# Filter rows by the parity of k2 already in batch 0: the filter re-arranged on chip, and the weight sums moved to VectorE

## The chip, the cores and the metric

The kernel runs on one core of a Trainium2 chip. The metric is the device time of one execution in microseconds (us). TensorE (PE) multiplies matrices, VectorE (DVE) and ScalarE (ACT) work on elements and empty PSUM, GpSimd (POOL) does small table work and issues the transfers that convert float32 to bfloat16, and SyncE (SP) issues the other transfers.

## The reference

For each of 8 batches of 3008 rows and 256 channels: a real FFT along the rows, a product with a filter per frequency and channel, the inverse FFT, and then two dense layers with an exact GELU between them.

```python
X = np.fft.rfft(x, axis=1)                       # x: (8, 3008, 256)
Y = X * (filt_r + 1j * filt_i)[None, :, :]       # filters: (1505, 256)
y = np.fft.irfft(Y, n=x.shape[1], axis=1)
h = y.reshape(24064, 256) @ w_in                 # w_in: (256, 2048)
g = 0.5 * h * (1.0 + erf(h / sqrt(2.0)))
out = g @ w_out                                  # w_out: (2048, 256)
```

## The kernel before

The FFT of 3008 points is split as 47 x 64. The frequency is k1 + 47 k2, and of k1 only 0 to 23 are kept; the conjugates stand in for the rest. A filter tile F holds, per partition, one k2 in 0 to 63 (direct rows 0 to 31, mirrored rows 32 to 63), and along the free dimension real or imaginary part, k1 and channel.

Batch 0 goes through the steps c1, c1t, c2, c3, c3t, c4 at the start, without DRAM between them. Its rows in F are needed twice, once for the real part of the data (partitions 0 to 63) and once for the imaginary part (64 to 127); `dup_filters` copies them. Batches 1 to 7 go through s1 to s4, which pass through DRAM (R1, R2) between the steps and are woven into the stream of the dense layers. They want F arranged in another way: even and odd k2 apart (parity 0 in partitions 0 to 63, parity 1 in 64 to 127), each twice. For this the kernel before saves F to DRAM and loads it again in the other order.

The stream has 47 tiles of 512 rows, 16 slots each. Slot jc of tile t does `mm1` (two matmuls and a GELU) for tile t and a sixteenth of the second product (`mm2`, or `mm2_seven`, a seven-product scheme that needs `weight_sums`) for tile t-1. Steps of the next batch are put into slots by number.

```python
    def load_filters(self, k0, k):

        nc, D = self.nc, self.D
        for t, src in enumerate((self.filt_r, self.filt_i)):
            direct = _dram(src, k0 * D, [[NA * D, 32], [D, k], [1, D]])
            mirror = _dram(src, (NA - k0) * D, [[NA * D, 32], [-D, k], [1, D]])
            for q, a in enumerate((direct, mirror)):
                nc.gpsimd.dma_start(out=self.F[32 * q:32 * q + 32, t, k0:k0 + k, :], in_=a)

    def save_filters(self):
        self.Fd = self.dram.tile([64, 2, K1, 256], BF16, tag="Fd", name="Fd")
        self.nc.sync.dma_start(out=self.Fd, in_=self.F[0:64])

    def load_filters_again(self, k0, k):

        for par in range(2):
            for r in range(2):
                for q in range(2):
                    o = 64 * par + 32 * r + 16 * q
                    self.nc.sync.dma_start(out=self.F[o:o + 16, :, k0:k0 + k, :],
                                           in_=self.Fd[32 * q + (par ^ q):32 * q + 32:2, :, k0:k0 + k, :])

    def dup_filters(self, eng, k0, k):
        for k in range(k0, k0 + k, 2):
            o, i = (self.F[r:r + 64, :, k:k + 2, :].rearrange("p t a b -> p t (a b)") for r in (64, 0))
            (eng.copy if eng is self.nc.scalar else eng.tensor_copy)(out=o, in_=i)

    # ...
    def table_2_parities(self):
        t = self.T2.rearrange("p k r (s j e) -> p k r s j e", s=2, e=2)
        for par in range(2):
            for q in range(2):
                self.nc.gpsimd.tensor_copy(out=self.T2p[:, :, par, :, q, :], in_=t[:, :, :, q, :, par ^ q])

    # ...
    def s1(self, b, c):

        nc = self.nc
        if c == 0:
            self.st[b, "R1"] = self.dram.tile([NB, 48, 256], BF16, tag="R1", name="R1")
        a = self.pa.tile([128, 2, 4, 256], BF16, tag="a", name="a_sb")
        x = self.st[b, "x"]
        ps = [[self.bank("ps_s1", "h" if i == h == 0 else "f") for h in range(2)] for i in range(2)]
        for i in range(2):
            for r in range(2):
                for h in range(2):
                    w = 8 * c + 4 * r + 2 * i
                    nc.tensor.matmul(ps[i][h][64 * r:64 * r + 64, :], lhsT=self.T1s[64 * h:64 * h + NA],
                                     rhs=x[64 * h:64 * h + NA, w:w + 2, :], start=True, stop=True)
        for i in range(2):
            for h in range(2):
                self._evac(a[:, h, 2 * i:2 * i + 2, :].rearrange("p a b -> p (a b)"), ps[i][h], "act" if h else False)
        o = self.st[b, "R1"].rearrange("n q c -> q n c")
        for r in range(2):
            for h in range(2):
                w = HB * h + 8 * c + 4 * r
                nc.sync.dma_start(out=o[:, w:w + 4, :], in_=a[64 * r:64 * r + 48, h])

    def r1(self, b, c):
        bt = self.pb.tile([128, 6, 256], BF16, tag="b", name="b_sb")
        self.st[b, "b", c] = bt
        v = self.st[b, "R1"].rearrange("n (r k) c -> (n r) k c", r=2)
        self.nc.sync.dma_start(out=bt, in_=v[:, 6 * c:6 * c + 6, :])


    def s2(self, b, p):
        nc = self.nc
        ps = self.bank("ps_s2")
        for i in range(2):
            k = 2 * p + i
            nc.tensor.matmul(ps[:, 256 * i:256 * i + 256], lhsT=self.T2p[:, k].rearrange("p a b c d -> p (a b c d)"),
                             rhs=self.st[b, "b", k // 6][:, k % 6, :], start=True, stop=True)
        w = self.st[b, "p", p] = self.pp.tile([128, 2, 512], BF16, tag="p12", name="p12")
        nc.vector.tensor_tensor(out=w, in0=ps.unsqueeze(1).to_broadcast([128, 2, 512]),

    # ... s3: matmuls over p, s3_out: results to DRAM (R2), r2: loads them, s4: last step, into the ring y
    def mm1(self, t, jc):
        nc = self.nc
        if jc == 0:
            self.st["g", t] = self.pg.tile([128, 16, TCH], FP16, tag="g", name="g_sb")
        ps = self.bank("ps_h", "h")
        o = 0
        for off, n in self.segs(t):
            for dc in range(2):
                nc.tensor.matmul(ps[:, o:o + n], lhsT=self.w_in_sb[:, dc, jc * 128:jc * 128 + 128],
                                 rhs=self.ring[:, dc, off:off + n], start=(dc == 0), stop=(dc == 1))
            o += n
        nc.scalar.activation(out=self.st["g", t][:, jc, :], in_=ps, func=AF.Gelu)

    # ...
    def weight_sums(self):

        w = self.w_out_sb.rearrange("p (i k) (n o) -> p k n i o", k=2, n=2)
        q, tt = self.w_sums, self.nc.gpsimd.tensor_tensor
        for o, a, b, op in ((q[:, 0], w[:, 0, 1], w[:, 0, 0], ALU.subtract), (q[:, 1], w[:, 1, 1], q[:, 0], ALU.add),
                            (q[:, 2], w[:, 1, 1], w[:, 0, 1], ALU.add), (q[:, 3], w[:, 1, 0], q[:, 1], ALU.subtract)):
            for i in range(0, 8, 2):
                tt(out=o[:, i:i + 2], in0=a[:, i:i + 2], in1=b[:, i:i + 2], op=op)
```

`table_4_all` makes, in 24 GpSimd products and sums of 96 x 376 elements, the table that s4 multiplies by; it needs `table_4_rows`, `weights_4` and `table_4_factors` before it. The start of the program and the schedule:

```python
    for k, n in ((0, 4), (4, 8), (12, 12)):
        m.load_filters(k, n)
    m.load_w_in()
    nc.gpsimd.memset(m.vt[:, :, 96, :], 0.0)
    m.dup_filters(nc.gpsimd, 4, 20)
    m.save_filters()
    # ... batch 0: c1 to c4; k1 = 0 to 3 duplicated on ACT and DVE; x of batch 1 and w_out loaded by GpSimd
    for b in range(1, B):
        hi = first(b)
        if b == 1:
            s1, n1, r1, s2, n2, group, r2, s4, n4 = 0, 4, 15, 25, 2.5, 12, 62, 70, 0.62
        else:
            s1, n1, r1, s2, n2, group, r2, s4, n4 = hi - 94, 3.7, hi - 80, hi - 71, 3.4, 14, hi - 25, hi - 17, 1
        unit = lambda p: s2 + group * (p // 4) + int(n2 * (p % 4))
        for u in range(16):
            put(s4 + int(u * n4), m.s4, b, u // 2, u % 2)
        for c in range(4):
            put(s1 + int(c * n1), m.s1, b, c)
            put(r1 if c < 3 else unit(3) + 1, m.r1, b, c)
            put(r2 if c < 3 else s4 + int(4 * n4) + 1, m.r2, b, c)
        for p in range(12):
            put(unit(p), m.s2, b, p)
            if p % 4 == 3:
                put(unit(p) + 3, m.s3, b, p // 4)
                put(unit(p) + 4, m.s3_out, b, p // 4, 1)
        if b + 1 < B:
            for i in range(8):
                put(unit(i + 2) if b > 1 else 25, m.load_next, b, i + 2, i // 2, i % 2)

    put(0, m.table_2_parities)
    put(1, m.table_u_pick, g)
    put(1, m.table_4_rows, g)
    put(1, m.weights_4, g)
    put(10, m.load_filters_again, 0, 8)
    put(16, m.load_filters_again, 8, 16)
    put(4, m.weight_sums)
    put(12, m.table_4_factors, g)
    put(14, m.table_u)
    put(15, m.table_4_all, g)
    # ... sums_1, sums_2, sums_3 for the seven-product scheme
    for s in range((NT + 1) * 16):
        t, jc = s // 16, s % 16
        for f, a in at.pop(s, ()):
            f(*a)
        if t >= 1:
            (m.mm2_seven if t - 1 in seven else m.mm2)(t - 1, jc)
        if t < NT:
            m.mm1(t, jc)
    assert not at
```

Of the kernel before, what the change touches and what calls it, by code (L numbers as in the profile page):

```python
# [18 lines left out]
NA, NB = 47, 64  # L19
# [11 lines left out]
class _Mix:  # L31
    def __init__(self, ctx, tc, x, filt_r, filt_i, w_in, w_out, out):
# [23 lines left out]
        self.T1 = c.tile([2 * NA, 96], BF16, name="T1")  # L56
        self.T2p = c.tile([128, K1, 2, 2, 2, 16], BF16, name="T2p")
        self.U = c.tile([128, 2, 2, HB], BF16, name="U")
# [29 lines left out]
    def load_filters(self, k0, k):  # L88

        nc, D = self.nc, self.D  # L90
        for t, src in enumerate((self.filt_r, self.filt_i)):
            direct = _dram(src, k0 * D, [[NA * D, 32], [D, k], [1, D]])
            mirror = _dram(src, (NA - k0) * D, [[NA * D, 32], [-D, k], [1, D]])
            for q, a in enumerate((direct, mirror)):
                nc.gpsimd.dma_start(out=self.F[32 * q:32 * q + 32, t, k0:k0 + k, :], in_=a)

    def save_filters(self):
        self.Fd = self.dram.tile([64, 2, K1, 256], BF16, tag="Fd", name="Fd")
        self.nc.sync.dma_start(out=self.Fd, in_=self.F[0:64])

    def load_filters_again(self, k0, k):

        for par in range(2):
            for r in range(2):
                for q in range(2):
                    o = 64 * par + 32 * r + 16 * q
                    self.nc.sync.dma_start(out=self.F[o:o + 16, :, k0:k0 + k, :],
                                           in_=self.Fd[32 * q + (par ^ q):32 * q + 32:2, :, k0:k0 + k, :])

# [95 lines left out]
    def signs(self, g):  # L205

        set_ = self.nc.vector.memset
        self.turn = [g.tile([128, 1], FP32, name=n) for n in ("turn_r", "turn_i")]
        for t, s in zip(self.turn, (-1.0, 1.0)):
            set_(t, s)  # L210
            for lo in (32, 96):
                set_(t[lo:lo + 32], -s)

        self.wtc = g.tile([128, 1], FP32, name="wtc")
        set_(self.wtc, 2.0)
        set_(self.wtc[0:4], 1.0)
# [14 lines left out]
    def unit_matrices(self, g, cols):  # L231
        ts = self.nc.vector.tensor_scalar
        self.eye, self.swap = (g.tile([128, 128], BF16, name=n) for n in ("eye", "swap"))
        sg, to = (g.tile([128, 1], FP32, name=n) for n in ("sg", "to"))

        ts(out=sg, in0=self.ri, scalar1=8.0, scalar2=-8.0 * TURNS - 1.0, op0=ALU.mult, op1=ALU.add)
        self.nc.vector.tensor_tensor(out=to, in0=self.p, in1=sg, op=ALU.add)
        ts(out=self.swap, in0=cols, scalar1=to, scalar2=sg, op0=ALU.is_equal, op1=ALU.mult)
        ts(out=self.eye, in0=cols, scalar1=self.p, scalar2=None, op0=ALU.is_equal)
# [6 lines left out]
    def table_2_swap(self, h):  # L246
        t2 = self.T2[:, 12 * h:12 * h + 12]
        for i in range(2):
            ps = self.bank("ps_sw", "n")
            self.nc.tensor.matmul(ps[:, 0:384], lhsT=self.swap, rhs=t2[:, :, 0, 32 * i:32 * i + 32],  # L250
                                  start=True, stop=True)
            self._evac(t2[:, :, 1, 32 * i:32 * i + 32], ps[:, 0:384].rearrange("p (k j) -> p k j", k=12),
                       "act", 1.0 - 2.0 * i)
# [56 lines left out]
    def table_2_parities(self):  # L310
        t = self.T2.rearrange("p k r (s j e) -> p k r s j e", s=2, e=2)
        for par in range(2):
            for q in range(2):
                self.nc.gpsimd.tensor_copy(out=self.T2p[:, :, par, :, q, :], in_=t[:, :, :, q, :, par ^ q])

# [7 lines left out]
    def table_u_pick(self, g):  # L323
        to = self.cols
        self.nc.gpsimd.iota(to, pattern=[[0, 2], [64, 2], [33, 2], [2, 16]], base=0, channel_multiplier=0,
                            allow_small_or_imprecise_dtypes=True)
        self.pick = g.tile([128, 128], BF16, name="pick")
        self.nc.gpsimd.tensor_scalar(out=self.pick, in0=to, scalar1=self.p, scalar2=None, op0=ALU.is_equal)
# [7 lines left out]
    def table_4_rows(self, g):  # L336
# [8 lines left out]
        t = self.T2.rearrange("p (a k) r j -> p r a j k", k=2)[:, 0, :, 0:2, :]  # L345
        for r in range(2):
# [28 lines left out]
    def s1(self, b, c):  # L375
# [13 lines left out]
        for i in range(2):  # L389
            for h in range(2):  # L390
                self._evac(a[:, h, 2 * i:2 * i + 2, :].rearrange("p a b -> p (a b)"), ps[i][h], "act" if h else False)
        o = self.st[b, "R1"].rearrange("n q c -> q n c")
# [12 lines left out]
    def s2(self, b, p):  # L405
        nc = self.nc
        ps = self.bank("ps_s2")
        for i in range(2):
            k = 2 * p + i
            nc.tensor.matmul(ps[:, 256 * i:256 * i + 256], lhsT=self.T2p[:, k].rearrange("p a b c d -> p (a b c d)"),  # L410
                             rhs=self.st[b, "b", k // 6][:, k % 6, :], start=True, stop=True)
# [194 lines left out]
    def weight_sums(self):  # L606

        w = self.w_out_sb.rearrange("p (i k) (n o) -> p k n i o", k=2, n=2)
        q, tt = self.w_sums, self.nc.gpsimd.tensor_tensor
        for o, a, b, op in ((q[:, 0], w[:, 0, 1], w[:, 0, 0], ALU.subtract), (q[:, 1], w[:, 1, 1], q[:, 0], ALU.add),  # L610
                            (q[:, 2], w[:, 1, 1], w[:, 0, 1], ALU.add), (q[:, 3], w[:, 1, 0], q[:, 1], ALU.subtract)):
            for i in range(0, 8, 2):
                tt(out=o[:, i:i + 2], in0=a[:, i:i + 2], in1=b[:, i:i + 2], op=op)

# [79 lines left out]
def kernel(  # L694
# [50 lines left out]
    m.dup_filters(nc.gpsimd, 4, 20)  # L745
    m.save_filters()

# [72 lines left out]
    def put(slot, f, *a):  # L820
        at.setdefault(slot, []).append((f, a))
# [34 lines left out]
    put(14, m.table_u)  # L856
    put(15, m.table_4_all, g)
    seven = range(1, NT - 1)
# [45 lines left out]
```

## Time and profile before

| | before |
|---|---|
| time, median of 3 runs | 761.4 us (761.34 to 761.51) |
| span of the profiled execution | 758.5 us, mean granted PE clock 0.995 |
| busy: ACT, share of the span | 72% |
| PE busy in 40 to 50, 60 to 70, 80 to 90 us | 7.24, 7.93, 8.18 of 10 us |
| granted PE clock in 50 to 60 and in 60 to 70 us | 0.83 |
| GpSimd's weight sums (L613) | 46.2 to 59.7 us |
| GpSimd's last product for s4's table (L373) | ends at 83.9 us |

A line of the profile names an engine, a source line of the kernel, an operation, and the tiles it writes and reads. "L410" is the matmul of s2, L413 its product with the filter, L387 s1's matmul, L396 its write to DRAM, L402 the load of b, L427 s3, L455 s4, L569 and L572 `mm1` and its GELU, L657 `mm2_seven`, L627 to L640 its sums, L673 one of its accumulations, L95 a filter load, L107 a reload, L113 a duplicating copy, L351 a matmul of `table_4_factors`. A row of windows gives a stretch, its length, then for PE, PEld (PE's weight loads), DVE, ACT and POOL the busy time and the number of instructions, then the granted PE clock, the busy share of the DMA engines and their GB/s. A row of waits gives who waited for whom, the total time, the number of times and the longest. A row of a timeline gives start, busy time, engine, line and operation, and in brackets the idle time before it and what ended that.

### The profile page before, as it was taken

Reading aid. Unit: us, or ns where it says so; the run is one execution under the profiler, and the core shown is the slowest. Engines: PE = TensorE matmul, PEld = TensorE weight load, DVE = VectorE, ACT = ScalarE, POOL = GpSimd, SP = SyncE. Lnnn points to the kernel's source line nnn. Section 1 sums busy time; section 2 is a strip of 40 time slices with the busy share of each in tenths; the row PEclk is TensorE's granted clock in tenths of the full one; section 3 lists DMA queues with packets and bytes.
Section 4 is the critical chain, followed back from the end, with each engine's and each line's share of the span. In section 5 each row is a group of like instructions: output and inputs, shape, how many; then the busy total and the mean of one; then the engine's idle time right before and its main releaser. Section 6 shows DMA issues by size and latency. Waiting matters only on the chain.

```text
span 758.5 us, 20181 instructions
## 1 busy us (share of the span) xinstructions
PE 741.2 (98%) x8388; PEld 519.3 (68%) x8388; DVE 581.4 (77%) x1043; ACT 547.6 (72%) x967; POOL 111.6 (15%) x207
## 2 busy tenths in 40 slices
PE   8988899999999999999999999999999999999998
PEld 4835567666777667666677666766677766777776
DVE  7935888799677986889777897779977799666562
ACT  7885567766787677867778667876678767777773
POOL 7969600021000210002000120001200000000000
PEclk9999999999999999999999999999999999999999
DMA  9999935555624745347525465254562432501011
GB/s 147 221 191 172 197 107 130 148 120 124 140 78 126 159 112 113 100 131 169 119 75 141 139 132 127 79 165 111 105 168 65 140 92 81 129 29 57 29 57 57
DMA packets 91500, 90.71 MB, mean 120 GB/s; under 512 B 7632, under 2 KB 78416, under 8 KB 91088
## 3 DMA queue, kind: packets, MB, share of 16 engines
q1 hardware_dynamic: 83024, 73.43, 36.2%
q0 software_dynamic: 8384, 16.00, 13.9%
q8 instruction: 65, 1.06, 0.6%
q14 instruction: 27, 0.22, 0.1%
HBM read 57.15 MB, written 48.23 MB: 139 GB/s over the span
## 4 chain that ended last, share of the span: by engine, by line
PE 85%; DVE 7%; DMA 4%; issue 1%; ACT 1%; POOL 0%; SPq 0%; DVEq 0%; ACTq 0%; POOLq 0%
PE ps_h L569 38%; PE ps_o L657 35%; PE ps_s L455 3%; PE ps_s L427 2%; DVE p L413 2%; DVE s_sb L627 2%; PE ps_s L410 2%; PE ps_s L387 2%; DMA b_sb<-R 2%; PE ps_o L596 1%; DMA R<-a_sb 1%; DMA x_sb<-in_x_dram 1%; PE ps_c L517 1%; ACT y_sb L295 1%; DVE ost L680 1%
## 5 line engine op out<-in xcount | busy, mean ns | idle before, releaser
L572 ACT ACTIVATE g_sb<-ps_h 128x512 f16<-128x512 f32 x752 | 448.2, 599 | 191.1 <-PE ps_h L569 188.7
L569 PE MATMUL ps_h<-y_sb,w_in_sb 128*128 128x512 bf16 (+3 forms) x1600 | 448.2, 368 | 1.3 <-ACT g_sb L572 0.8
L657 PEld LDWEIGHTS <-g_sb 128*128 128x128 f16 x2880 | 190.3, 98 | 81.7 <-issue 16.9
L657 PEld LDWEIGHTS <-s_sb 128*128 128x128 f16 x2160 | 147.3, 98 | 51.3 <-issue 3.3
L569 PEld LDWEIGHTS <-w_in_sb 128*128 128x128 bf16 x1600 | 125.2, 98 | 9.3 <-issue 3.6
L657 PE MATMUL ps_o<-w_sums,g_sb 128*128 128x128 f16 x1440 | 125.0, 219 | 2.2 <-DVE t_sb L673 1.5
L657 PE MATMUL ps_o<-w_sums,s_sb 128*128 128x128 f16 x1440 | 124.5, 219 | 0.0
L627 DVE TENSOR_TENSOR s_sb<-g_sb 128x1024 f16<-128x1024 f16 x180 | 121.4, 697 | 0.0
L413 DVE TENSOR_TENSOR p<-ps_s,F 128x1024 bf16<-128x1024 f32 x84 | 102.6, 1221 | 23.2 <-PE ps_s L410 15.8
L657 PE MATMUL ps_o<-w_out_sb,g_sb 128*128 128x128 f16 x1440 | 118.4, 219 | 0.4
L118 POOL COPY gate<-p 1x1 bf16<-1x1 bf16 x40 | 19.4, 484 | 415.3 <-DVE p L413 415.3
L633 DVE TENSOR_TENSOR g_sb<-s_sb,g_sb 128x1024 f16<-128x1024 f16 x90 | 62.3, 693 | 1.1
L657 PE MATMUL ps_o<-w_out_sb,s_sb 128*128 128x128 f16 x720 | 62.2, 219 | 0.0
L640 DVE TENSOR_TENSOR s_sb<-g_sb 128x1024 f16<-128x1024 f16 x90 | 61.5, 683 | 0.0
L299 DVE TENSOR_SCALAR y_sb<-ps_s 128x376 bf16<-128x376 f32 x56 | 30.6, 546 | 28.9 <-PE ps_s L455 28.9
L297 DVE CAST a_sb<-ps_s 128x512 bf16<-128x512 f32 x56 | 36.1, 686 | 18.6 <-PE ps_s L387 15.4
L455 PEld LDWEIGHTS <-d_sb 96*128 96x128 bf16 x448 | 31.2, 98 | 26.4 <-issue 1.9
L675 DVE TENSOR_TENSOR t_sb<-t_sb,ps_o 128x256 f32<-128x256 f32 x45 | 18.7, 416 | 38.5 <-PE ps_o L657 38.5
L672 DVE TENSOR_TENSOR ost<-t_sb,ps_o 128x256 f32<-128x256 f32 x45 | 18.9, 419 | 31.2 <-PE ps_o L657 31.2
L680 DVE TENSOR_TENSOR ost<-t_sb,ps_o 128x256 f32<-128x256 f32 x90 | 33.7, 416 | 6.8 <-PE ps_o L657 6.8
L455 PE MATMUL ps_s<-T4a,d_sb 96*128 96x94 bf16 x448 | 37.1, 206 | 1.0 <-DMA d_sb<-R 0.9
L410 PE MATMUL ps_s<-b_sb,T2p 128*128 128x256 bf16 x168 | 32.3, 274 | 2.1 <-DMA b_sb<-R 2.1
(149 smaller groups left out, 524.3 us busy)
## 6 DMA issues: line engine op xcount, KB each, us to landing
out_dram<-ost SPq DMA_DIRECT2D x93, 256.0 KB, 2.7
x_sb<-in_x_dram POOLq DMA_DIRECT2D x64, 188.0 KB, 3.6
R<-a_sb SPq DMA_DIRECT2D x112, 96.0 KB, 2.2
b_sb<-R SPq DMA_DIRECT2D x28, 384.0 KB, 4.4
R<-v_sb SPq DMA_DIRECT2D x84, 128.0 KB, 2.4
d_sb<-R SPq DMA_DIRECT2D x56, 192.0 KB, 3.9
F<-Fd SPq DMA_DIRECT2D x8, 256.0 KB, 12.1
Fd<-F SPq DMA_DIRECT2D x1, 1536.0 KB, 9.9
```

The lines of the kernel that those rows point to most:

```text
L297: self.nc.vector.tensor_copy(out=out, in_=in_)
L299: self.nc.vector.tensor_scalar(out=out, in0=in_, scalar1=scale, scalar2=None, op0=ALU.mult)
L410: nc.tensor.matmul(ps[:, 256 * i:256 * i + 256], lhsT=self.T2p[:, k].rearrange("p a b c d -> p (a b c d)"), rhs=self.st[b, "b", k // 6][:, ...
L413: nc.vector.tensor_tensor(out=w, in0=ps.unsqueeze(1).to_broadcast([128, 2, 512]), in1=self.F[:, :, 2 * p:2 * p + 2, :].rearrange("p t a b ...
L455: nc.tensor.matmul(ps[:, 94 * i:94 * i + 94], lhsT=d[:, (grp % 2) * 4 + i, 128 * half:128 * half + 128], rhs=self.T4a[:, 4 * grp + i], sta ...
L569: nc.tensor.matmul(ps[:, o:o + n], lhsT=self.w_in_sb[:, dc, jc * 128:jc * 128 + 128], rhs=self.ring[:, dc, off:off + n], start=(dc == 0), ...
L572: nc.scalar.activation(out=self.st["g", t][:, jc, :], in_=ps, func=AF.Gelu)
L627: self.nc.vector.tensor_tensor(out=self.st["s", t][:, i:i + 2], in0=a, in1=b, op=ALU.subtract)
L633: self.nc.vector.tensor_tensor(out=a21[:, k], in0=self.st["s", t][:, k, 0], in1=a22[:, k], op=ALU.add)
L640: self.nc.vector.tensor_tensor(out=self.st["s4", t][:, k], in0=a12[:, k], in1=s2[:, k], op=ALU.subtract)
L657: nc.tensor.matmul(ps[:, (m + 1) % 2, sub, :], lhsT=a[:, i, 128 * sub:128 * sub + 128], rhs=b[:, i], start=i == 0, stop=i == 7)
L680: v(out=c(h, 1 - h), in0=tt, in1=p, op=ALU.add)
```

## The change

The filter is loaded with the parities apart from the start: partitions 0 to 31 hold even k2, 32 to 63 odd k2, direct and mirrored rows alternating. Table T2 takes the same order of k2, so that batch 0 works with it. For batches 1 to 7 the halves only need to move by blocks of 32 partitions, which is done on chip: by VectorE for k1 below 8, by transfers inside SBUF for the rest. The DRAM copy, its save and its reloads go. The mirrored rows of the two parities are loaded apart, so that each load has three transfers where it had two. The weight sums go from GpSimd to VectorE, the GpSimd table work comes earlier, one of two ScalarE evacuations of s1 in batch 1 goes to VectorE, and batch 1's s2, r2 and s4 come three slots earlier, with s4 spread over a little more time.

```diff
# ... (layout of one table or index to match)
@@ -89,23 +89,23 @@
 
         nc, D = self.nc, self.D
         for t, src in enumerate((self.filt_r, self.filt_i)):
-            direct = _dram(src, k0 * D, [[NA * D, 32], [D, k], [1, D]])
-            mirror = _dram(src, (NA - k0) * D, [[NA * D, 32], [-D, k], [1, D]])
-            for q, a in enumerate((direct, mirror)):
-                nc.gpsimd.dma_start(out=self.F[32 * q:32 * q + 32, t, k0:k0 + k, :], in_=a)
-
-    def save_filters(self):
-        self.Fd = self.dram.tile([64, 2, K1, 256], BF16, tag="Fd", name="Fd")
-        self.nc.sync.dma_start(out=self.Fd, in_=self.F[0:64])
-
-    def load_filters_again(self, k0, k):
-
-        for par in range(2):
-            for r in range(2):
-                for q in range(2):
-                    o = 64 * par + 32 * r + 16 * q
-                    self.nc.sync.dma_start(out=self.F[o:o + 16, :, k0:k0 + k, :],
-                                           in_=self.Fd[32 * q + (par ^ q):32 * q + 32:2, :, k0:k0 + k, :])
+            for q, par, n in ((0, 0, 32), (1, 0, 16), (1, 1, 16)):
+                if q:
+                    a = _dram(src, ((2 - par) * NA - k0) * D, [[2 * NA * D, n], [-D, k], [1, D]])
+                else:
+                    a = _dram(src, k0 * D, [[NA * D, 2], [2 * NA * D, 16], [D, k], [1, D]])
+                nc.gpsimd.dma_start(out=self.F[HB * par + q:HB * par + 2 * n:2, t, k0:k0 + k, :], in_=a)
+
+    def parities_outside(self, k0, k):
+
+        step = 4 if k0 == 0 else k
+        for k in range(k0, k0 + k, step):
+            for o, i in ((64, 32), (32, 0)):
+                o, i = (self.F[r:r + 32, :, k:k + step, :].rearrange("p t a b -> p t (a b)") for r in (o, i))
+                if k0 == 0:
+                    self.nc.vector.tensor_copy(out=o, in_=i)
+                else:
+                    self.nc.sync.dma_start(out=o, in_=i)
 
     def dup_filters(self, eng, k0, k):
         for k in range(k0, k0 + k, 2):
@@ -205,12 +205,6 @@
     def signs(self, g):
 
         set_ = self.nc.vector.memset
-        self.turn = [g.tile([128, 1], FP32, name=n) for n in ("turn_r", "turn_i")]
-        for t, s in zip(self.turn, (-1.0, 1.0)):
-            set_(t, s)
-            for lo in (32, 96):
-                set_(t[lo:lo + 32], -s)
-
         self.wtc = g.tile([128, 1], FP32, name="wtc")
         set_(self.wtc, 2.0)
         set_(self.wtc[0:4], 1.0)
@@ -235,6 +229,9 @@
 
         ts(out=sg, in0=self.ri, scalar1=8.0, scalar2=-8.0 * TURNS - 1.0, op0=ALU.mult, op1=ALU.add)
         self.nc.vector.tensor_tensor(out=to, in0=self.p, in1=sg, op=ALU.add)
+        self.turn = [g.tile([128, 1], FP32, name=n) for n in ("turn_r", "turn_i")]
+        for t, s in zip(self.turn, (-1.0, 1.0)):
+            ts(out=t, in0=sg, scalar1=s, scalar2=None, op0=ALU.mult)
         ts(out=self.swap, in0=cols, scalar1=to, scalar2=sg, op0=ALU.is_equal, op1=ALU.mult)
         ts(out=self.eye, in0=cols, scalar1=self.p, scalar2=None, op0=ALU.is_equal)
 
@@ -247,9 +244,9 @@
         t2 = self.T2[:, 12 * h:12 * h + 12]
         for i in range(2):
             ps = self.bank("ps_sw", "n")
-            self.nc.tensor.matmul(ps[:, 0:384], lhsT=self.swap, rhs=t2[:, :, 0, 32 * i:32 * i + 32],
+            self.nc.tensor.matmul(ps[:, 0:384], lhsT=self.swap, rhs=t2[:, :, 0, i::2],
                                   start=True, stop=True)
-            self._evac(t2[:, :, 1, 32 * i:32 * i + 32], ps[:, 0:384].rearrange("p (k j) -> p k j", k=12),
+            self._evac(t2[:, :, 1, i::2], ps[:, 0:384].rearrange("p (k j) -> p k j", k=12),
                        "act", 1.0 - 2.0 * i)
 
 
@@ -308,10 +305,9 @@
             v.tensor_copy(out=self.T1s[r:r + NA, 0:48], in_=self.T1[0:NA, 0:48])
 
     def table_2_parities(self):
-        t = self.T2.rearrange("p k r (s j e) -> p k r s j e", s=2, e=2)
         for par in range(2):
-            for q in range(2):
-                self.nc.gpsimd.tensor_copy(out=self.T2p[:, :, par, :, q, :], in_=t[:, :, :, q, :, par ^ q])
+            for k in range(0, K1, 12):
+                self.nc.gpsimd.tensor_copy(out=self.T2p[:, k:k + 12, par], in_=self.T2[:, k:k + 12, :, HB * par:HB * par + HB])
 
     def table_u_rows(self, g):
 
# ... (layout of one table or index to match)
@@ -388,7 +384,8 @@
                                      rhs=x[64 * h:64 * h + NA, w:w + 2, :], start=True, stop=True)
         for i in range(2):
             for h in range(2):
-                self._evac(a[:, h, 2 * i:2 * i + 2, :].rearrange("p a b -> p (a b)"), ps[i][h], "act" if h else False)
+                self._evac(a[:, h, 2 * i:2 * i + 2, :].rearrange("p a b -> p (a b)"), ps[i][h],
+                           "act" if h and (b > 1 or i) else False)
         o = self.st[b, "R1"].rearrange("n q c -> q n c")
         for r in range(2):
             for h in range(2):
# ... (layout of one table or index to match)
@@ -606,11 +603,10 @@
     def weight_sums(self):
 
         w = self.w_out_sb.rearrange("p (i k) (n o) -> p k n i o", k=2, n=2)
-        q, tt = self.w_sums, self.nc.gpsimd.tensor_tensor
+        q, tt = self.w_sums, self.nc.vector.tensor_tensor
         for o, a, b, op in ((q[:, 0], w[:, 0, 1], w[:, 0, 0], ALU.subtract), (q[:, 1], w[:, 1, 1], q[:, 0], ALU.add),
                             (q[:, 2], w[:, 1, 1], w[:, 0, 1], ALU.add), (q[:, 3], w[:, 1, 0], q[:, 1], ALU.subtract)):
-            for i in range(0, 8, 2):
-                tt(out=o[:, i:i + 2], in0=a[:, i:i + 2], in1=b[:, i:i + 2], op=op)
+            tt(out=o, in0=a, in1=b, op=op)
 
     def quarters(self, t):
 
@@ -717,9 +713,9 @@
     m.load_x(0, 8, 8, (0,))
     m.kk = m.iota(g, "kk", [128, 6], [[1, 6]])
     m.jj = g.tile([128, NB], FP32, name="jj")
-    for sgn, lo, base in ((1, 0, 0), (-1, 32, m.S - NA)):
-        nc.gpsimd.iota(m.jj[:, lo:lo + 32], pattern=[[sgn * NA, 32]], base=base,
-                       channel_multiplier=0, allow_small_or_imprecise_dtypes=True)
+    for q, (sgn, base) in enumerate(((1, 0), (-1, m.S - 2 * NA))):
+        nc.gpsimd.iota(m.jj.rearrange("p (a i q) -> p q a i", a=2, q=2)[:, q], pattern=[[NA, 2], [2 * NA * sgn, 16]],
+                       base=base, channel_multiplier=0, allow_small_or_imprecise_dtypes=True)
     m.load_x(0, 8, 8, (1,))
     cols = m.cols = m.iota(g, "cols", [128, 128], [[1, 128]])
     m.load_x(0, 16, 16)
@@ -743,7 +739,6 @@
 
     nc.gpsimd.memset(m.vt[:, :, 96, :], 0.0)
     m.dup_filters(nc.gpsimd, 4, 20)
-    m.save_filters()
 
 
     m.table_2_sin(0)
@@ -826,7 +821,7 @@
     for b in range(1, B):
         hi = first(b)
         if b == 1:
-            s1, n1, r1, s2, n2, group, r2, s4, n4 = 0, 4, 15, 25, 2.5, 12, 62, 70, 0.62
+            s1, n1, r1, s2, n2, group, r2, s4, n4 = 0, 4, 15, 22, 2.5, 12, 59, 67, 0.75
         else:
             s1, n1, r1, s2, n2, group, r2, s4, n4 = hi - 94, 3.7, hi - 80, hi - 71, 3.4, 14, hi - 25, hi - 17, 1
         unit = lambda p: s2 + group * (p // 4) + int(n2 * (p % 4))
@@ -845,16 +840,17 @@
             for i in range(8):
                 put(unit(i + 2) if b > 1 else 25, m.load_next, b, i + 2, i // 2, i % 2)
 
+    put(0, m.table_4_rows, g)
+    put(0, m.weights_4, g)
+    put(0, m.table_u_pick, g)
     put(0, m.table_2_parities)
-    put(1, m.table_u_pick, g)
-    put(1, m.table_4_rows, g)
-    put(1, m.weights_4, g)
-    put(10, m.load_filters_again, 0, 8)
-    put(16, m.load_filters_again, 8, 16)
-    put(4, m.weight_sums)
-    put(12, m.table_4_factors, g)
-    put(14, m.table_u)
-    put(15, m.table_4_all, g)
+    put(7, m.table_4_factors, g)
+    put(11, m.table_u)
+    put(11, m.table_4_all, g)
+    put(14, m.parities_outside, 0, 8)
+    put(18, m.weight_sums)
+    put(16, m.parities_outside, 8, 8)
+    put(17, m.parities_outside, 16, 8)
     seven = range(1, NT - 1)
     for t in seven:
         for i, s in enumerate((12, 13, 15, 17)):
```

More of the change, by code (lines that the diff above doesn't have):

```diff
@@ L56, in __init__ @@
         self.T1 = c.tile([2 * NA, 96], BF16, name="T1")
-        self.T2p = c.tile([128, K1, 2, 2, 2, 16], BF16, name="T2p")
+        self.T2p = c.tile([128, K1, 2, 2, HB], BF16, name="T2p")
         self.U = c.tile([128, 2, 2, HB], BF16, name="U")
@@ L324, in table_u_pick @@
         to = self.cols
-        self.nc.gpsimd.iota(to, pattern=[[0, 2], [64, 2], [33, 2], [2, 16]], base=0, channel_multiplier=0,
+        self.nc.gpsimd.iota(to, pattern=[[0, 2], [64, 2], [1, HB]], base=0, channel_multiplier=0,
                             allow_small_or_imprecise_dtypes=True)
@@ L344, in table_4_rows @@
                 v.tensor_copy(out=self.T1g[:, x, r], in_=t.unsqueeze(2).to_broadcast([NA, 12, 2, 2]))
-        t = self.T2.rearrange("p (a k) r j -> p r a j k", k=2)[:, 0, :, 0:2, :]
+        t = self.T2.rearrange("p (a k) r j -> p r a j k", k=2)[:, 0, :, 0:NB:HB, :]
         for r in range(2):
@@ L409, in s2 @@
             k = 2 * p + i
-            nc.tensor.matmul(ps[:, 256 * i:256 * i + 256], lhsT=self.T2p[:, k].rearrange("p a b c d -> p (a b c d)"),
+            nc.tensor.matmul(ps[:, 256 * i:256 * i + 256], lhsT=self.T2p[:, k].rearrange("p a b c -> p (a b c)"),
                              rhs=self.st[b, "b", k // 6][:, k % 6, :], start=True, stop=True)
```

## The prediction

> **What bounds the kernel now.** I read the page's busy times first, then windows by stage, then TensorE's (PE's) waits, then the timelines of the engines that end them.
>
> ```profile
> PE 741.2 (98%) x8388; PEld 519.3 (68%) x8388; DVE 581.4 (77%) x1043; ACT 547.6 (72%) x967; POOL 111.6 (15%) x207
> ...
> 0.00:38.50 38.50, 34.16 (x428) 25.08 (x428) 32.80 (x79) 30.99 (x56) 31.84 (x62) 1.00 0.98 184
> 38.50:71.90 33.40, 28.57 (x174) 15.19 (x173) 12.59 (x16) 22.42 (x46) 26.32 (x47) 0.90 1.00 187
> 71.90:100.00 28.10, 24.73 (x266) 16.21 (x264) 24.54 (x35) 16.27 (x28) 15.63 (x20) 1.00 0.86 180
> 100.00:120.00 20.00, 19.09 (x237) 13.56 (x236) 14.65 (x29) 14.32 (x26) 0.00 (x0) 1.00 0.54 133
> 120.00:758.00 638.00, 634.68 (x7297) 449.30 (x7294) 496.80 (x888) 463.59 (x814) 37.83 (x80) 1.00 0.44 109
> ```
>
> PE is the bound. From 120 us on it is busy 634.7 of 638.0 us, and nothing in that stretch changes, so the change can act only on the first 120 us: batch 0 (to 38.5), MoE tiles 0 and 1 (to 71.9), tile 2 and after. There PE idles 4.3, 4.8, 3.4 and 0.9 us, and the granted clock falls to 0.90 in the second stretch. This is the whole stock to be won. PE's waits name it:
>
> ```profile
> PE ps_s L410 <- DMA b_sb<-R: 2.1, 1, 2.1
> PE ps_t L351 <- ACT a_sb L295: 1.9, 1, 1.9
> ...
> PE ps_o L657 <- DVE t_sb L673: 1.5, 1, 1.5
> ...
> PE ps_s L455 <- DMA d_sb<-R: 0.9, 1, 0.9
> ```
>
> The first is batch 1's s2, which waits for b; the second is the fourth s1, whose evacuation waits for a write of a_sb to DRAM, with PE stuck behind it. The third comes from VectorE (DVE) running late. The queue of SyncE shows what the reload of the filter does to b:
>
> ```profile
> 49.69 4.04 SPq L107 DMA_DIRECT2D F<-Fd  x8
> 53.83 2.76 SPq L396 DMA_DIRECT2D R<-a_sb  x4
> 59.99 1.29 SPq L402 DMA_DIRECT2D b_sb<-R  x3
> 61.38 4.63 SPq L107 DMA_DIRECT2D F<-Fd  x8
> ```
>
> The last a_sb was evacuated by 50.1, but its writes go out at 53.83, behind eight filter reloads. b is asked for at 59.99 and lands at 63.2. The second reload lands as late as 16.5 us after issue (the longest of the F tile's transfers): DVE sits idle until 82.57, when it multiplies p of k = 8, 9, and the DVE waits between 78 and 97 us follow from that queue.
>
> [...] after each wait of about 2 us the clock is 0.83 over 10 us, which is 3.4 us at half speed, some 1.7 us of PE work; after the wait of 1.5 us at 84 it is not seen. [...] L627 takes up to 1.34 us while GpSimd (POOL) works, against a mean of 0.697. [...] The new direct filter load has a first dimension of 2 in place of 32 [...]
>
> **The change part by part.**
>
> (1) Filter loads: 12 POOL transfers become 18 of the same total bytes. This is the part that costs:
>
> ```profile
> 13.79 1.10 POOL L95 DMA_DIRECT2D F<-in_filt_r_dram  x2
> 14.89 1.10 POOL L95 DMA_DIRECT2D F<-in_filt_i_dram  x2
> 15.98 1.13 POOL L129 DMA_DIRECT2D w_in_sb<-in_moe_w_in_dram  x2
> 17.09 0.19 POOL L744 MEMSET vt_sb<- 128x64 bf16 x1
> 18.12 3.97 POOL L113 COPY F<-F 64x1024 bf16<-64x1024 bf16 x4 [0.84 <-DMA F<-in_filt_i_dram]
> ```
>
> One issue takes 0.53 us, so six take 3.2. POOL is free at 17.28 now and waits 0.84 us for data; it would be free at 20.5, and the duplicating copies would start there: 2.4 us late. DVE needs a copy (1.0 us each) before each product (1.14 us apart). Products now run back to back from 18.16 to the end of batch 0, the third at 19.3 right after the first copy. So nothing swallows the delay: **+2.4 us** on the start of the stream. [...] I put in **+0.8**.
>
> (2) Save (1.5 MB) and reloads (16 transfers, 3 MB) go; four 256 KB copies inside SBUF come, and four DVE copies of 32x2048 bf16. A DVE copy of 1024 elements took 0.42 us, so I estimate 0.7 us each, 2.8 in all, at slot 14, where DVE now idles 9.8 us. The SBUF transfers are two chains of two; [...] k = 8 is first used at slot 34, near 68: just hidden. Without eight issues (4.0 us) ahead, the last writes go out as soon as a_sb is ready.
>
> (3) In batch 1 one of two ACT evacuations of each s1 goes to DVE. Tile 0 is paced by ACT: four GELUs and two evacuations repeat every 2.86 us, 0.48 per instruction. Five take 2.4, three times before the last s1: **-1.4 us**. DVE then does 3 x 0.65 us in 2.4.
>
> (4) The last s1's wait of 1.9: its a_sb buffer is free only when the first write has landed (48.8). The write's own time stays (7.1 us in the chain: the x and w_out loads fill the queues, busy share 1.0 until 51 with or without the save, since those loads also start 2.4 later). But s1 comes at about 48.5, so 0.5 remains, and the table operations no longer stand behind it. **-1.4**, and the half clock (some 1.5 of 1.7, as part of it lies in ACT's time): **-1.5**.
>
> (5) s2's wait of 2.1. After: last evacuation 51.6, four writes issued 1.4, landed 2.2 later, b 3.2: 58.5. Slot 22 comes at 51.2 + 6 x 0.87 = 56.4. So moving s2 three slots forward spends what the freed queue gives, and 1.5 to 2 us of wait stay, with a half clock likely: **-0.5**.
>
> (6) Weight sums: 16 POOL instructions of 0.67 us become four DVE instructions of 128x1024, 0.7 each, up to 1.3 against POOL. With 5.9 us of waiting for w_out and 10.7 of work gone, the table products on POOL start near 47 in place of 59.7 and end near 70 in place of 83.9, so DVE is slowed less in tile 2; and there is no late reload to wait for. The waits of 78 to 97 us (0.4 + 1.5 + 0.8 + 0.6 = 3.3) shrink to about 1: **-2.2**. Against it, DVE has up to 5 us of copies and 5 of sums between 51 and 61, and may be behind when s2 begins: **+0.5**.
>
> (7) s4's wait of 0.9: write, read and slots keep their distances. 0. GpSimd's table copies, the strided swap and the two `turn` instructions on DVE are fractions of a microsecond beside other work. 0.
>
> Sum: 2.4 + 0.8 - 1.4 - 1.4 - 1.5 - 0.5 - 2.2 + 0.5 = -3.3. I lean a little further, as (5) may go better: 757.5 us.
>
> **The rivals.** *All stalls vanish and the loads cost nothing*: PE's idle time and half clocks of 38.5 to 100 are 8.2 + 3.4, and ACT's relief beside them: about 749. For it: every one of these stalls is tied to the removed traffic or to POOL. Against it: POOL's queue before 18.12, which had 0.84 us of slack and gets 3.2 us more. *The opening becomes the bound*: [...] the first and last groups land 2 to 3 us late, the start slips by 5 us and the total is 760 to 763. [...] *DVE becomes the bound of tile 1*: copies and sums queue ahead of s2's products; a wait of s3 for p (0.8 now) grows to 2 or 3 and the gain of (6) is gone: about 760. Against: DVE idles 9.8 us in that place today. *The transfers were hidden anyway*: then only (1) would show, 763; but PE's two longest waits speak against it.
>
> **Range and chances.** From 752 (stalls gone, start 2 us late) to 763 (start slips and the wait at s2 stays). 2% is 15.2 us; the whole stock of idle time before 120 us, 13.4 us, is less, so faster by 2% has 2%, and slower by 2% would need 15 us of new stalls: 1%.
>
> **What would show it.** (1): POOL's first duplicating copy near 20.5, the first s1 near 41. (3): s1s about 2.4 us apart. (4): PE's wait at the last s1 under 1 us and the clock 1.00 there. (5): `ps_s <- b_sb` still 1.5 us or more. (6): table products ending near 70, no DVE idle time near 80. It is wrong if POOL's copies start at 18 as before, if b arrives before slot 22, or if s3 waits for DVE by more than 1.5 us.

## The result, and the profile after

The changed kernel takes 762.6 us (median of 4 runs, 761.58 to 763.98) against 761.45 before: a ratio of 1.0015, 95% interval 0.9996 to 1.0033. That is no difference that these runs can tell from zero, where 757.5 had been predicted. The page's busy times, the window of the opening as before, and the three stages behind it, shifted by the 11 us that they come later:

```profile
PE 742.7 (98%) x8388; PEld 521.1 (68%) x8388; DVE 591.6 (78%) x1051; ACT 545.8 (72%) x963; POOL 106.6 (14%) x197
...
0.00:38.50 38.50, 27.03 (x254) 18.39 (x255) 23.76 (x61) 21.76 (x35) 25.55 (x49) 0.87 0.73 109
...
49.40:82.80 33.40, 30.72 (x217) 16.63 (x215) 28.04 (x33) 22.72 (x46) 30.55 (x35) 0.95 0.79 180
82.80:110.90 28.10, 28.10 (x314) 19.23 (x312) 26.11 (x43) 19.71 (x35) 2.73 (x6) 1.00 0.59 133
110.90:130.90 20.00, 19.77 (x253) 14.38 (x251) 15.22 (x31) 15.59 (x31) 0.00 (x0) 1.00 0.54 132
```

Two opposite things happened. In the first 38.5 us PE is busy 27.0 us where it was 34.2, and the DMA engines' busy share fell from 0.98 to 0.73: the opening is starved. Behind it PE is busy 6.2 us more than before in the same three stages (78.59 us in place of 72.39), and the clock in the first of them is 0.95 where it was 0.90. PE's waits, in which L492 is batch 0's c2, L407 s2, L566 `mm1` and L452 s4, say the same:

```profile
PE ps_c L492 <- DVE p L496: 7.2, 2, 6.8
PE ps_s L407 <- DMA b_sb<-R: 2.0, 1, 2.0
...
PE ps_s L452 <- DMA d_sb<-R: 0.9, 3, 0.4
...
PE ps_h L566 <- DVE a_sb L294: 0.7, 1, 0.7
```

The waits of tile 2 are gone, the one of the fourth s1 is down from 1.9 to 0.7 and stands at `mm1` now, the one at s2 is as long as it was, and a new one of 6.8 us stands in batch 0. The cut is the first matmul of s1: it starts at 38.48 us before and at 49.44 after, 11.0 us late. From there to the end the span holds 720.0 us before (758.5 - 38.5) and 712.1 after (761.5 - 49.4): **11.0 lost in the opening, 7.9 gained behind it**. The 7.9 agree with the windows: 6.2 us less idle time, and 3.3 us less at half clock (a granted clock of 0.50; 0.95 for 0.90 as the mean of 33.4 us), which I estimate at 1.7 from that mean. The sum of 3.1 is that of two profiled executions; the medians differ by 1.15.

The loss is in the filter loads. GpSimd's timeline (L97 is a filter load, L113 a duplicating copy) shows it waiting again and again for an earlier filter load before it can issue the next; and then for data:

```profile
16.67 1.13 POOL L97 DMA_DIRECT2D F<-in_filt_r_dram  x2
20.22 0.54 POOL L97 DMA_DIRECT2D F<-in_filt_r_dram  x1 [2.42 <-DMA F<-in_filt_r_dram]
20.75 1.13 POOL L97 DMA_DIRECT2D F<-in_filt_i_dram  x2
23.54 0.54 POOL L97 DMA_DIRECT2D F<-in_filt_i_dram  x1 [1.66 <-DMA F<-in_filt_i_dram]
...
25.92 3.97 POOL L113 COPY F<-F 64x1024 bf16<-64x1024 bf16 x4
33.70 5.95 POOL L113 COPY F<-F 64x1024 bf16<-64x1024 bf16 x6 [3.81 <-DMA F<-in_filt_i_dram]
```

The copies, which began at 18.12 and 22.38 before, begin at 25.92 and 33.70. The chain of the work that ended last, from 6 to 35 us, is three filter transfers end to end, where before it ran through the work of PE, VectorE and ScalarE from 11 us on:

```profile
6.43 7.83 DMA F<-in_filt_r_dram
...
15.05 8.20 DMA F<-in_filt_i_dram
...
23.54 10.05 DMA F<-in_filt_i_dram
```

SyncE's queue (L393 writes a_sb, L399 loads b, L108 is a transfer inside SBUF) is as foreseen: the writes of a_sb go out in one run, nothing stands between them and b, and the SBUF transfers come after:

```profile
51.80 11.26 SPq L393 DMA_DIRECT2D R<-a_sb  x16
64.91 1.29 SPq L399 DMA_DIRECT2D b_sb<-R  x3
66.44 10.24 SPq L108 DMA_DIRECT2D F<-F  x4
```

### The profile page after: what moved, and what is told of

It reads as the page before. It is cut to its first block, busy times and chain, and to the rows that moved or that the text cites. A ratio compares the mean times of both kernels' runs of the same rounds, so it can differ in the third digit from the quotient of the medians.

```text
span 761.5 us, 20156 instructions
## 1 busy us (share of the span) xinstructions
PE 742.7 (98%) x8388; PEld 521.1 (68%) x8388; DVE 591.6 (78%) x1051; ACT 545.8 (72%) x963; POOL 106.6 (14%) x197
## 4 chain that ended last, share of the span: by engine, by line
PE 84%; DMA 8%; DVE 4%; ACT 1%; POOL 1%; issue 1%; SPq 1%; DVEq 0%; ACTq 0%; POOLq 0%
PE ps_h L566 38%; PE ps_o L653 34%; PE ps_s L424 3%; PE ps_s L452 3%; DMA F<-in_filt_i_dram 2%; PE ps_s L407 2%; PE ps_s L383 2%; DVE p L410 2%; DMA R<-v_sb 1%; DMA d_sb<-R 1%; PE ps_o L593 1%; DVE s_sb L623 1%; DMA R<-a_sb 1%; DMA F<-in_filt_r_dram 1%; ACT g_sb L569 1%
## 5 line engine op out<-in xcount | busy, mean ns | idle before, releaser
L566 PE MATMUL ps_h<-y_sb,w_in_sb 128*128 128x512 bf16 (+3 forms) x1600 | 446.8, 367 | 0.7 <-DVE a_sb L294 0.7
L566 PEld LDWEIGHTS <-w_in_sb 128*128 128x128 bf16 x1600 | 124.8, 98 | 7.6 <-issue 2.0
L294 DVE CAST a_sb<-ps_s 128x512 bf16<-128x512 f32 x60 | 38.5, 686 | 16.4 <-PE ps_s L383 13.9
L452 PEld LDWEIGHTS <-d_sb 96*128 96x128 bf16 x448 | 31.4, 98 | 27.1 <-issue 1.4
L452 PE MATMUL ps_s<-T4a,d_sb 96*128 96x94 bf16 x448 | 37.4, 206 | 0.9 <-DMA d_sb<-R 0.9
L407 PE MATMUL ps_s<-b_sb,T2p 128*128 128x256 bf16 x168 | 32.2, 273 | 2.0 <-DMA b_sb<-R 2.0
```

The costliest lines, as they stand in the source:

```text
L294: self.nc.vector.tensor_copy(out=out, in_=in_)
L452: nc.tensor.matmul(ps[:, 94 * i:94 * i + 94], lhsT=d[:, (grp % 2) * 4 + i, 128 * half:128 * half + 128], rhs=self.T4a[:, 4 * grp + i], sta ...
```

## The experiments

Each is set against the kernel before on the same chip. As the time of a run mixes opening and stream, the table splits the profiled span at the first s1. Kernels whose stream is the old one show 720.0 to 722.7 there, so differences below about 3 us between single profiles decide nothing.

| kernel | first s1, us | from there to the end | time, us | ratio to before (95%) |
|---|---|---|---|---|
| before | 38.5 | 720.0 | 761.45 | |
| after | 49.4 | 712.1 | 762.6 | 1.0015 (0.9996 to 1.0033) |
| e1_direct_16 | 43.0 | 710.9 | 755.65, one run | |
| e2_mirror_halves | 40.8 | 721.6 | 764.16, one run | |
| e3_direct_2x16 | 44.5 | 721.2 | 767.49, one run | |
| e4_every_second_row | 38.0 | 721.1 | 760.84, one run | |
| e7_direct_16x2 | 38.2 | 722.7 | 762.72, one run | |
| n1_old_loads | 38.5 | 712.3 | 752.68 | 0.9887 (0.9862 to 0.9911) |
| n2_slots_25 | 39.2 | 710.4 | 750.62 | 0.9860 (0.9836 to 0.9885) |
| n3_sums_gpsimd | 38.0 | 714.8 | 754.39 | 0.9905 (0.9876 to 0.9934) |
| n4_act_evacuates | 39.0 | 713.3 | 753.28 | 0.9896 (0.9861 to 0.9930) |
| n5_only_filter | 41.3 | 713.9 | 752.98 | 0.9904 (0.9868 to 0.9940) |
| n5_again | 38.6 | 713.1 | 753.02 | 0.9888 (0.9871 to 0.9904) |
| n6_slots_26_71 | 40.1 | 710.5 | 750.04 | 0.9859 (0.9840 to 0.9878) |

The first s1 of unchanged loads also moves from run to run (38.0 to 41.3), so a shift of less than 3 us there needs a second witness.

### Why the filter loads are slow

Four kernels, and then a fifth, tell three theories apart: the first dimension of 2 in a load's source (A), the number of transfers (B), the stride of two partitions (C).

**e1_direct_16.** The changed kernel; in `load_filters`:

```diff
-            for q, par, n in ((0, 0, 32), (1, 0, 16), (1, 1, 16)):
+            for q, par, n in ((0, 0, 16), (0, 1, 16), (1, 0, 16), (1, 1, 16)):
                 # mirrored source as in the changed kernel
-                    a = _dram(src, k0 * D, [[NA * D, 2], [2 * NA * D, 16], [D, k], [1, D]])
+                    a = _dram(src, (par * NA + k0) * D, [[2 * NA * D, n], [D, k], [1, D]])
```

> The changed kernel, with each direct filter load split into its two parities: two transfers of 16 rows in place of one whose first dimension is 2. 24 filter transfers in all, the same rows in the same places. Theory A [...]: the data land at the old rate and only the queue of GpSimd counts; twelve more issues than the kernel before, 12 x 0.53 = 6.4 us, less its 0.84 us of slack: first s1 at about 38.5 + 5.6 = 44, against 49.4 in the changed kernel, and a time of about 757. Rival B (the number of transfers and their waits for a free place are the cost): 24 are worse than 18, first s1 at 52 or later, time 765 or more. Rival C (writing every second partition is slow): first s1 unchanged at 49 or later, since these still write every second partition.

Measured: first s1 at 43.0, time 755.65. More transfers make it 6.4 us faster at the first s1 and 7 in time, with every second partition still written. B and C fall as the main cause.

**e2_mirror_halves.** The kernel before, with the mirrored load as two of 16 rows, `[[NA * D, 16], [-D, k], [1, D]]` each:

> The kernel before, with each mirrored filter load cut into two transfers of 16 rows: 18 transfers, as many as in the changed kernel, but all with a first dimension of 16 or 32 and neighbouring partitions. Theory A: only the six extra issues show, 6 x 0.53 = 3.2 less 0.84 of slack: first s1 at about 41, time about 763.5. Rival B (the number of transfers): as in the changed kernel, first s1 near 49 and, with the old stream, 772.

Measured: first s1 at 40.8 (2.3 later), 764.16. The second witness is GpSimd's first copy, which begins at 20.50, where step 1 of the prediction had 20.5, and all ten copies then run without a wait:

```profile
20.50 9.88 POOL L113 COPY F<-F 64x1024 bf16<-64x1024 bf16 x10
```

Eighteen transfers with a first dimension of 16 or 32 cost the six issues and no more.

**e3_direct_2x16.** The kernel before, one line:

```diff
-            direct = _dram(src, k0 * D, [[NA * D, 32], [D, k], [1, D]])
+            direct = _dram(src, k0 * D, [[NA * D, 2], [2 * NA * D, 16], [D, k], [1, D]])
```

> The kernel before, with the source of the direct filter loads read as 2 x 16 rows (even k2, then odd) in place of 32: 12 transfers, neighbouring partitions, the mirrored loads untouched. The direct filter rows stand in another order than the tables expect, so the output is that of a filter with permuted rows. Theory A: the direct loads alone make the start late, first s1 at 46 or later, time 769 or more, and the direct loads take about twice as long to land or more. Rivals B and C: no difference, first s1 at 38.5, time 761.5.

Measured: first s1 at 44.5, 6.0 later, with only the direct loads touched; 767.49. A little less than A's figure, but B and C, which wanted 38.5, are out.

**e4_every_second_row.** The kernel before, with `self.F[q:64:2, ...]` as the destination in place of `self.F[32 * q:32 * q + 32, ...]`:

> The kernel before, with the same 12 filter transfers written to every second partition (direct to the even ones, mirrored to the odd ones). The filter rows stand in another order than the tables expect, so the output is that of a filter with permuted rows. Theory A: no difference, first s1 at 38.5, time 761.5. Rival C (every second partition is slow): first s1 several us later, at 43 or more, time 766 or more.

Measured: first s1 at 38.0, 760.84. No cost of the stride is seen, in the start or in the landing (5.5 us for the real part's largest loads, as before); C is out.

**e7_direct_16x2.** This left one rival: a source of four dimensions could be slow as such. As e3, with the dimensions exchanged:

```diff
-            direct = _dram(src, k0 * D, [[NA * D, 2], [2 * NA * D, 16], [D, k], [1, D]])
+            direct = _dram(src, k0 * D, [[NA * D, 16], [16 * NA * D, 2], [D, k], [1, D]])
```

> As e3_direct_2x16, but the source of the direct filter loads is read as 16 x 2 rows in place of 2 x 16: the same number of dimensions, transfers, bytes and pieces, only the first dimension is 16. (The direct rows again stand in another order than the tables expect, so the output is that of a filter with permuted rows.) Theory A [...]: as the kernel before, first s1 within 1 us of 38.5, and the 192 KB direct loads land in about 6 us and not 11. Rival (a source of four dimensions is slow whatever its first one): as e3_direct_2x16, first s1 at 44 or later.

Measured: first s1 at 38.2. The transfers' rows (line, queue, number, size, median us to landing) for the real part's largest loads, direct and mirrored together, in e3_direct_2x16:

```profile
F<-in_filt_r_dram POOLq DMA_DIRECT2D x2, 192.0 KB, 11.4
```

and in e7_direct_16x2, where they are those of the kernel before:

```profile
F<-in_filt_r_dram POOLq DMA_DIRECT2D x2, 192.0 KB, 5.5
```

Same bytes, pieces, number of dimensions and transfers; 2 or 16 in front makes 11.4 or 5.5 us. The order of the addresses differs too, but e1_direct_16 reads rows two apart as e3 does, with 16 in front, and its loads of 96 KB land in 3.9. What lies behind the difference, no run here shows.

### What the rest of the change gives

**n1_old_loads.** The changed kernel with the loads, T2 and signs of the kernel before. Each pair of neighbouring rows then holds one row that the parity wants and one that it does not; the wanted row is copied over the other, inside SBUF, in place:

```diff
+    def pair_rows(self, k0, k):
+        for par in range(2):
+            for q in range(2):
+                o, s = 64 * par + 32 * q, par ^ q
+                self.nc.sync.dma_start(out=self.F[o + 1 - s:o + 32:2, :, k0:k0 + k, :],
+                                       in_=self.F[o + s:o + 32:2, :, k0:k0 + k, :])
     # table_2_parities, real and imaginary part side by side:
+            for q in range(2):
+                t = self.T2[:, :, :, 32 * q + (par ^ q):32 * q + 32:2]
+                self.nc.gpsimd.tensor_copy(out=self.T2p[:, :, par, q], in_=t.rearrange("p k r i -> p k i r"))
     # schedule
-    put(14, m.parities_outside, 0, 8)
-    put(16, m.parities_outside, 8, 8)
-    put(17, m.parities_outside, 16, 8)
+    put(1, m.pair_rows, 0, 8)
+    put(16, m.pair_rows, 8, 16)
```

> The changed kernel with the filter loads and row order of the kernel before (12 transfers, natural order of k2), so that batch 0 starts as before. For batches 1 to 7 the rows are made ready inside SBUF by four transfers per range of k1 that copy every second row onto its neighbour (real and imaginary part then stand side by side; the table T2p and the choice of U take the same order). No DRAM copy, no VectorE copies of the filter; all else as in the changed kernel. Theory A (the loads are the whole loss; the rest of the change gains what the traces show after the first s1, 720.0 - 712.1 = 7.9 us): first s1 at 38.5, time about 752 to 754. Rival D (the gain after the first s1 exists only because the late start leaves the transfer queues empty): first s1 at 38.5, the wait of the fourth s1 for its buffer back at 1.5 or more, time 756 or more.

Measured: first s1 at 38.5, 712.3 behind it, 752.68: as theory A expected. Rival D is out: `mm1` waits 0.9 behind the fourth s1, and the gain does not need a late start.

**n2_slots_25.** One line of n1: batch 1's `s2, ..., r2, s4, n4` back to `25, ..., 62, 70, 0.62`.

> As n1_old_loads, with s2, r2 and s4 of batch 1 back at the slots of the kernel before (25, 62, 70, spread 0.62). Step 5 of the prediction (moving s2 three slots forward spends what the freed queue gives, and leaves a wait of 1.5 to 2 with a half clock): here b has landed before slot 25, no wait at s2, and the time is 2 to 3.5 us shorter than n1_old_loads. Rival (the three slots are worth something because later steps need the room): same or longer, by 0 to 2 us.

Measured: 750.62 (750.14 to 751.36) against 752.68 (752.37 to 753.05): 2.1 us shorter without the move of s2, r2 and s4 (all three go back together). PE's wait at s2 in n1_old_loads:

```profile
PE ps_s L406 <- DMA b_sb<-R: 3.4, 1, 3.4
```

and in n2_slots_25:

```profile
PE ps_s L406 <- DMA b_sb<-R: 0.8, 1, 0.8
```

The granted clock over 38.5 to 71.9 us is 0.95 in the first and 1.00 in the second. Not all was won: s4 waits 2.0 for d in n2.

**n3_sums_gpsimd.** n1 with `weight_sums` on `nc.gpsimd` in 16 instructions at slot 4.

> As n1_old_loads, with the weight sums back on GpSimd in 16 instructions at slot 4. Step 6 of the prediction (the sums hold up the table products on GpSimd, which slow VectorE in tile 2, worth about 2): table products end some 10 us later than in n1_old_loads, and the time is 1 to 3 us longer. Rival (the late waits came from the reload of the filter, which is gone here; the sums on GpSimd cost nothing, and VectorE is even freer): within 0.5 us, or shorter.

Measured: 754.39 (752.14 to 755.37), 1.7 longer by the medians, but the times overlap with n1's; behind the first s1 2.5 longer. The last table sum on GpSimd, in n1_old_loads and then in n3_sums_gpsimd:

```profile
66.74 0.98 POOL L368 TENSOR_TENSOR T4a<-t_sb 96x376 bf16<-96x376 f32 x1
```

```profile
79.96 0.98 POOL L368 TENSOR_TENSOR T4a<-t_sb 96x376 bf16<-96x376 f32 x1
```

Thirteen microseconds later on GpSimd. PE waits 1.2 us for g_sb from VectorE in n3 and not at all in n1, which is the mechanism of step 6; that it costs time is not settled by the overlapping times.

**n4_act_evacuates.** n1 with `"act" if h else False` in s1.

> As n1_old_loads, with two evacuations of each s1 of batch 1 on ScalarE as in the kernel before. Step 3 of the prediction (ScalarE paces tile 0; worth 1.4): the fourth s1 comes 1 to 1.5 us later than in n1_old_loads and the time is about 1.4 longer. Rival (the write of the first a_sb decides when the fourth s1 can go on, so a faster ScalarE only waits there): fourth s1 later, but within 0.5 us in time.

Measured: the fourth s1 comes 9.0 us after the first in place of 8.1, yet the time is 753.28 (752.42 to 755.27), 0.6 longer and overlapping. The times don't tell the two apart, but the traces speak for the rival. ScalarE's evacuation of the fourth s1, in n1_old_loads and then in n4_act_evacuates:

```profile
48.62 0.60 ACT L290 ACTIVATE a_sb<-ps_s 128x512 bf16<-128x512 f32 x1 [1.11 <-DMA R<-a_sb]
```

```profile
49.44 1.08 ACT L290 ACTIVATE a_sb<-ps_s 128x512 bf16<-128x512 f32 x2 [0.40 <-DMA R<-a_sb]
```

Both wait for the write of the first a_sb and begin 10.2 and 10.4 us after the first s1 (38.45 and 38.99). Of the 0.9 us by which the fourth s1 is earlier, 0.3 at most are left there.

**n5_only_filter and n5_again.** The kernel before with nothing but `pair_rows` (slots 10 and 16) for the save and the reloads, and T2p and U in the order of n1. The two are the same kernel.

> The kernel before, with nothing changed but the way to the second filter order: the save to DRAM and its 16 reloads go, eight transfers inside SBUF come at the same slots, that copy every second row onto its neighbour (T2p and the choice of U take the same order). Loads, weight sums, GpSimd's order, ScalarE's evacuations and all slots as before. Step 2 of the prediction (the reloads hold up the last writes of a_sb and keep p of k = 8, 9 waiting): PE's wait at s2 falls from 2.1 to about 0.5 or less and VectorE's idle time near 80 us goes; the fourth s1 still waits about 1.9. Time 754 to 757. Rival (what GpSimd, VectorE and ScalarE share out in the rest of the change is the source of the gain, and the transfers were hidden): within 1.5 us of 761.4.

> n5_only_filter once more, with more rounds, because its four times spread from 750.65 to 756.95. If the removed DRAM trip is worth what its profile shows after the first s1 (720.0 - 713.9 = 6.1 us): 754 to 755. If the rest of the change adds nothing to it but the cost of the moved slots: 752 to 753.

Measured: 752.98 (750.65 to 756.95), and again 753.02 (751.65 to 753.83), a little better than 754 to 757. PE's wait at s2 is 0.4 and 0.3, and VectorE has no idle time near 80 us. The wait at the fourth s1 was expected to stay at 1.9; it fell as well, to 0.8 and 1.2. In n5_again:

```profile
PE ps_t L346 <- ACT a_sb L290: 1.2, 1, 1.2
...
PE ps_s L406 <- DMA b_sb<-R: 0.3, 1, 0.3
```

The DRAM trip alone is worth about 1.1%, as much as n1 with all the rest of the change. Behind the first s1 it is 6.1 and 6.9 us.

**n6_slots_26_71.** n2 with `26, ..., 62, 71, 0.62`.

> As n2_slots_25, with s2 at slot 26 and s4 at slot 71 (r2 stays at 62), because there PE still waited 0.8 at s2 and 2.0 at s4. If these two waits cost what they show: s2's wait 0, s4's 1.2 or less, time 1 to 2 us below n2_slots_25, about 749. If the waits only move: within 0.5 us of it.

Measured: 750.04 (749.78 to 752.42) against 750.62 (750.14 to 751.36), not told apart; s2 still waits 0.4 and s4 2.0, where 0 and at most 1.2 had been expected. n2 and n6 are the best versions here, 1.4% below the kernel before.

## Why the prediction was wrong

**Step 1 failed, in its second term**, the +0.8 for the direct loads, which was my estimate and rested on no measured number. The six issues were right: 2.4 expected, 2.3 measured in e2. The shape was worth 6.0 alone (e3), and both together 11.0. The first sign, a first copy near 20.5, came at 25.92. The 2.7 us that are left over are no more than the openings of unchanged loads vary by; a part of them can be read in the trace. While it issues filter loads, GpSimd waits 3.0 us in all for earlier transfers before the change, 2.8 in e2 (more transfers), 3.5 in e3 (slow ones) and 7.4 after (both), so slow loads seem to hold up more issues when there are more of them. That was not tested by itself. The pace of the x loads of 47 rows (188 KB in 3.6 us, the median before) says nothing of a first dimension of 2. The prediction had a rival in which loads land 2 to 3 us late, the start slips by 5 us and the total is 760 to 763, and still entered slow loads in the sum at 0.8. That 762.6 falls into the rival's range is luck: the start slipped by 11, and the rest gained more than the rival allowed.

**Steps 2 to 7 held in their sum, with errors that nearly cancel.** They summed to -6.5; behind the first s1 the traces show -7.9. The shares were not as foreseen: most of it comes with the filter's way alone.

- Step 2 is the core: with the DRAM trip gone and nothing else (n5, by other copies than those of the change) about 6 to 7 of the 7.9. That the transfers had been hidden anyway, another rival, is out. The DVE copies took 1.18 us each, 4.72 in all, and not 0.7; GpSimd was at work beside them. The four SBUF transfers landed 3.0 to 5.3 us after their issue. Copies and transfers were hidden all the same, for PE waited for no product of batch 1.
- Step 3: -1.4 expected. The three gaps between the first and the fourth s1 take 8.1 us in place of 8.5. The first is 2.4, as predicted; in the other two ScalarE now also has evacuations of the tables. What is won mostly ends in the wait for the first write of a_sb (n4), so the step was sized too high; what is left of it in time stays open.
- Step 4: the wait fell from 1.9 to 0.7 and the clock over 50 to 60 us is 1.00. Right in size; but n5_again, with neither a later start nor the table work moved, has 1.2 there, so part of it goes with the DRAM trip.
- Step 5: the wait of 2.0 with a lowered clock (0.91 over 60 to 80 us) came as predicted, 0.1 less than before and not 0.5. n2 makes the judgement sharper: on the healthy start the move costs 2.1 us.
- Step 6: the waits of tile 2 are gone, 3.3 us and not 2.2. About half of that belongs to the vanished reload, since n5 keeps the sums on GpSimd and has 1.5 to 1.6 of such waits. The table products end 32 us after the first s1, where about 29 was expected. VectorE was busy from 59.4 to 73.9 us without a break and the first product of s2 came 2.7 us after its matmul had begun, but PE did not wait for it: the rival in which VectorE bounds tile 1 did not come about.

Put together: the steps' sum of -3.3, plus the 7.8 us that step 1 was short (11.0 - 3.2), less 1.4 of the others, is +3.1, the difference of the two profiles. The medians of the runs differ by 1.15; the 2 us between are within what single profiles and the opening vary by. That the two kernels come out equal is a coincidence of two sizes.

## What to carry to other kernels

When a load is reordered, look at the first dimension of its source pattern (the side tried here), not only at bytes, pieces and number of transfers: the same 32 rows read as 16 x 2 or 2 x 16 differ by a factor of two in landing (5.5 and 11.4 us). Here a delay of GpSimd's last copies by 11.3 us (22.38 to 33.70) went into the start of the stream in full, while the gain behind it was collected wait by wait; so cut the trace at the point where the two meet and sum each side. And move a consumer forward only as far as its data come forward: the three slots took back what a freed queue had given.

## What the runs showed of the hardware

PE's half clock, a granted clock of 0.50, did not grow in step with the wait. By windows of 1 us it lasted about 3.4 us after waits of 1.9 and 2.1 us (before) and of 2.0 (after). The mean clock gives the same for n1 (0.96 and 0.87 over 50 to 60 and 60 to 70 us, with a wait of 3.4) and about 3.3 us for n4 (0.95 over 33.4 us, with a wait of 2.5). Around the wait of 6.8 us in batch 0 of the changed kernel it lasted three times as long:

```profile
24.00:34.10 10.10, 5.83 (x40) 4.63 (x41) 4.71 (x4) 2.11 (x3) 5.71 (x9) 0.50 0.92 138
```

For waits of 1.5 to 2 us it came or did not. After a wait of 1.5 us, e3 has four `mm1` matmuls that took 1.91 us from 56.88 on, as long as the four at a clock of 0.50 from 50.72 on in the kernel before; after its own wait of 1.5 us, the kernel before shows a clock of 1.00. Waits of 2.0 us in n5_again (at s4) and n6 (in batch 0) left the mean clock of the whole span at 1.000. Four VectorE sums of 128x1024 took 1.20 to 1.35 us beside GpSimd's products; a sum of that size took 0.68 at 81.65 us, after the last of these products, but one at 76.33 took 0.68 too, beside a GpSimd instruction that took 1.43 in place of 0.98.
